# Four of eight first loads split into 120 and 8 partitions, in a kernel of windowed attention and a gated MLP block

## The chip, the core and the metric

The kernel runs on one core of a Trainium2 chip. The metric is the time of one execution on the device in microseconds (us): before the change 156.29, the median of three runs (155.95 to 157.16).

A core has five instruction streams. TensorE (PE) multiplies matrices and also transposes them against an identity. VectorE (DVE), ScalarE (ACT) and GpSimd (POOL) do elementwise work; GpSimd also issues transfers that convert float32 to bf16 on the way. SyncE (SP) does nothing here but issue plain transfers. All transfers, whoever issues them, are carried by the same sixteen DMA engines.

## What is computed

Attention in which each row sees the first four positions (the sinks) and a window of 128, then a gated MLP in which a 768x768 matrix mixes the positions:

```python
B, H, S, D = 4, 8, 768, 64
scores = q @ k^T / sqrt(D)
keep = (pos_k < 4) | (0 <= pos_q - pos_k < 128)
a = softmax(where(keep, scores, -1e9))
x = (a @ v)                         # heads side by side: (4, 768, 512)
h = gelu_tanh(x @ w_in)             # 512 -> 1024
u, v = h[..., :512], h[..., 512:]
v_n = layernorm(v) * g_ln
v_s = w_sg @ v_n + b_sg             # over the 768 positions
out = x + (u * v_s) @ w_out
```

## The kernel before

The order of all work is written out by hand, in one long list of steps (STEPS); each name calls a small function, its numbers say for which batch and tile, and a last letter says on which engine. Each engine runs its own steps in that order. A step starts when its engine has reached it and its inputs are there. The four batches overlap: while the MLP of one batch runs, the attention of the next is mixed in. Steps on PE that wait for nothing (WARM and HM.n, n products of a tile of zeros) fill its early gaps.

The change touches the loads of q and k of the first batch. They come as plain float32 transfers issued by SP, one for each pair of heads: LPQ.g and LPK.g, g from 0 to 3. Each moves 128 partitions times two heads times 384 numbers: 256 pieces of 1,536 bytes, 393 KB. Within one transfer a partition holds six neighbouring positions of two heads. The pairs 0 and 1 lie in the tile uT, the pairs 2 and 3 in the tile z, which are free at that time. SP's own order is q0, k0, k1, q1, q2, LG (g_ln, four partitions), k2, k3, q3, and then LC: four small transfers that fetch the sink rows of v into the tile vs, eight partitions each. After them SP has nothing to do until the transposes of the second batch.

What follows each load: a cast to bf16 (CPQ and CPK; ACT for q0, k0 and k2, GpSimd for k1 and k3, DVE for q1, q2 and q3), transposes on PE (TQ and TK), a copy out of PSUM (EQ and EK on ACT or DVE), the scores (QK), the exponentials (EX), the masks (MK) and the product with v (AV), which is normalised by NR. On GpSimd the cast of k1 stands ahead of LVH.0.0 and LVH.0.1, the two transfers that bring v of the first batch; the cast of k3 follows, and then the loads of the second batch's q and k and of the weights: LW (w_in), LWS (w_sg), and much later LWO (w_out), first needed by OU, the last product of the first batch. GpSimd's loads of q, k and v write pieces of 128 bytes.

SP's transfers share eight completion counters in turn, so each transfer from the ninth on waits until the one eight places before it on SP has landed. Before the change the ninth is q3, which waits for q0; then the four transfers of LC wait for k0, k1, q1 and q2. GpSimd's transfers have eight counters of their own.

Of the kernel before, what the change touches and what calls it, by code (L numbers as in the profile page):

```python
# [14 lines left out]
HOW = "GBBC"  # L15
VHOW = "HHHH"
BIG = 1e9


STEPS = """  # L20
# [55 lines left out]
def kernel(  # L76
# [14 lines left out]
    nc = tc.nc  # L91
# [48 lines left out]
    z = Ring("z", 2, [128, NT, d_half], BF16)  # L140
# [96 lines left out]
    def pair(key, g):  # L237
        both = uT.get(("f", g)).rearrange("p c s -> p (c s)") if g < 2 else z.get(("f", g)).rearrange("p t d -> p (t d)")
        i = "qk".index(key)
        return both.bitcast(F32)[:, S * i:S * (i + 1)]  # L240

    def load_pair(key, src, g):
        return nc.sync.dma_start(out=pair(key, g).rearrange("p (h f) -> p h f", h=2),
                                 in_=src[0, 2 * g:2 * g + 2].rearrange("h (p t) d -> p h (t d)", p=128))

    def LPQ(g):
        return load_pair("q", q, g)

    def LPK(g):
        return load_pair("k", k, g)  # L250
# [78 lines left out]
    def MASK0():  # L329
        nc.vector.tensor_copy(mask0, mask1)  # L330
        nc.vector.memset(mask0[0:n_sink, 0:256], 1.0)
        for m, bias in ((mask0, bias0), (mask1, bias1)):
            nc.vector.tensor_scalar(out=bias, in0=m, scalar1=-1.0, scalar2=BIG, op0=ALU.add, op1=ALU.mult)

# [376 lines left out]
```

## Time and profile before

| | us |
|---|---|
| median of three runs | 156.29 |
| the profiled execution, its time | 157.69 |
| its span, from the first to the last instruction | 156.0 |
| PE busy | 146.7 (94%) |
| DVE busy | 123.4 (79%) |
| ACT busy | 99.0 (64%) |
| GpSimd busy | 99.3 (64%) |
| granted TensorE clock | 1.0 throughout |
| moved by SP's queue | 13.41 MB |
| moved by GpSimd's queue | 11.01 MB |

The profiled execution took 1.69 us more than its own span. A line of the profile names the engine, the source line, the operation, and the tiles as output<-inputs. "Idle before" is how long the engine stood still ahead of an instruction, and the arrow names what ended the wait. A name with a small q behind the engine (SPq) is the engine's sequencer, here issuing transfers. Beside the summary, the trace holds when each transfer's completion counter rose. A transfer over 128 partitions raises its counter sixteen times, once for each DMA engine when its share has landed; these times come without the engine's name, sorted. A transfer has landed with its last count.

### The profile page before, as it was taken

The numbers are of one execution on the slowest core, as the hardware profiler recorded it, in microseconds if no ns is written. First come the engines' busy times: TensorE is split into PE (matmuls) and PEld (weight loads), VectorE is DVE, ScalarE is ACT, GpSimd is POOL, SyncE is SP. The second block draws the span as 40 slices with busy tenths as digits, with TensorE's granted clock in tenths as the row PEclk, the third lists the DMA queues.
The fourth block names the chain that finished last, engine by engine and source line by source line (L and its number), as shares of the span: only waits on it lengthen the run. The fifth ranks groups of instructions, "written<-read, shape, count | busy, mean of one in ns | idle before, by whom it ended". The sixth has DMA issues, their size and how long they took to land.

```text
span 156.0 us, 3856 instructions
## 1 busy us (share of the span) xinstructions
PE 146.7 (94%) x1549; PEld 94.2 (60%) x1549; DVE 123.4 (79%) x295; ACT 99.0 (64%) x110; POOL 99.3 (64%) x127
## 2 busy tenths in 40 slices
PE   6988989999999979989999999999999999999990
PEld 2445577779675756747566764486567644776530
DVE  4557789829989969969789887899789956867981
ACT  3699798799899846276897855269954025591000
POOL 4099779388999899997549869640798610300400
PEclk9999999999999999999999999999999999999999
DMA  4999999999999999999999199995710580510064
GB/s 156 282 365 151 153 197 189 166 192 193 146 143 142 193 152 139 167 156 156 168 230 246 22 285 174 178 197 60 236 71 3 102 235 0 202 63 11 0 227 179
DMA packets 86170, 24.67 MB, mean 158 GB/s; under 512 B 78660, under 2 KB 83016, under 8 KB 86152
## 3 DMA queue, kind: packets, MB, share of 16 engines
q0 software_dynamic: 64608, 11.01, 94.9%
q1 hardware_dynamic: 21544, 13.41, 33.1%
q8 instruction: 12, 0.20, 0.5%
q14 instruction: 6, 0.05, 0.1%
HBM read 24.81 MB, written 6.29 MB: 199 GB/s over the span
## 4 chain that ended last, share of the span: by engine, by line
PE 73%; DMA 17%; DVE 2%; POOL 2%; issue 1%; ACT 1%; SPq 1%; ACTq 0%
PE mm L622 17%; PE mm L639 14%; PE sc L561 13%; PE sc L602 12%; DMA w_out_sb<-in_moe_w_out_dram 7%; DMA v_sb<-in_v_dram 6%; PE sc L478 4%; DMA uT<-in_k_dram 4%; PE mm L519 3%; PE mm L377 3%; PE mm L523 2%; PE mm L526 2%; PE mm L614 1%; POOL v_sb L269 1%; PE mm L545 1%
## 5 line engine op out<-in xcount | busy, mean ns | idle before, releaser
L483 ACT ACTIVATE P<-sc 128x1024 bf16<-128x1024 f32 (+1 forms) x48 | 43.4, 953 | 10.3 <-PE sc L478 10.1
L622 PE MATMUL mm<-wsgT,z 128*128 128x384 bf16 x192 | 34.1, 327 | 0.0
L622 PEld LDWEIGHTS <-z 128*128 128x128 bf16 x192 | 17.7, 98 | 11.9 <-issue 0.7
L639 PE MATMUL mm<-w_out_sb,wsg_gated 128*128 128x512 bf16 x96 | 22.7, 379 | 1.1 <-DMA w_out_sb<-in_moe_w_out_dram 1.1
L561 PE MATMUL sc<-w_in_sb,xT 128*128 128x512 bf16 x96 | 22.2, 379 | 0.7 <-ACT vt L565 0.7
L627 DVE SCALAR_TENSOR_TENSOR gtmp<-mm,g_sb,b_bc 128x384 bf16<-128x384 f32 x32 | 19.1, 611 | 4.2 <-PE mm L622 3.6
L602 PE MATMUL sc<-xT,w_in_sb 128*128 128x256 bf16 x192 | 22.1, 273 | 0.0
L493 POOL TENSOR_SCALAR_AFFINE_SELECT P<-P 128x512 bf16<-128x512 bf16 x21 | 14.0, 667 | 12.3 <-ACT P L483 12.0
L632 POOL TENSOR_TENSOR wsg_gated<-gtmp,uT 128x384 bf16<-128x384 bf16 x15 | 14.5, 982 | 10.9 <-DVE gtmp L627 10.9
L574 DVE BATCH_NORM_STATS2 st<-vt 128x6 f32<-128x512 f32 x24 | 15.4, 685 | 7.5 <-ACT vt L565 7.4
L602 PEld LDWEIGHTS <-w_in_sb 128*128 128x128 bf16 x192 | 18.7, 98 | 3.0
L536 DVE TENSOR_TENSOR x_sb<-mm,rcp 128x384 bf16<-128x384 f32 (+1 forms) x36 | 18.5, 513 | 1.2
L643 DVE TENSOR_TENSOR ot<-mm,x_sb 128x512 f32<-128x512 f32 x24 | 16.1, 684 | 2.7 <-PE mm L639 2.5
L565 ACT ACTIVATE vt<-sc 128x1024 f32<-128x1024 f32 x12 | 12.3, 1027 | 9.0 <-PE sc L561 8.9
L583 POOL TENSOR_TENSOR rs<-rs,neg_half 128x4 f32<-128x4 f32 (+1 forms) x8 | 6.9, 867 | 17.4 <-DVE rs L578 16.0
L223 POOL DMA_DIRECT2D k<-in_k_dram x18 | 16.4, 928 | 0.7 <-DMA v_sb<-in_v_dram 0.7
L223 POOL DMA_DIRECT2D q<-in_q_dram x18 | 16.7, 952 | 0.0
L519 PE MATMUL mm<-v_sb,P 128*128 128x65 bf16 x192 | 15.9, 194 | 0.7 <-DMA v_sb<-in_v_dram 0.6
L519 PEld LDWEIGHTS <-P 128*128 128x128 bf16 x192 | 14.5, 98 | 2.8 <-issue 0.6
L639 PEld LDWEIGHTS <-wsg_gated 128*128 128x128 bf16 x96 | 9.2, 98 | 11.4 <-DMA w_out_sb<-in_moe_w_out_dram 1.4
L561 PEld LDWEIGHTS <-xT 128*128 128x128 bf16 x96 | 9.2, 98 | 10.9 <-issue 0.9
L478 PE MATMUL sc<-qT,kT 64*128 64x128 bf16 (+1 forms) x256 | 14.8, 238 | 0.6 <-DVE qT L198 0.3
(90 smaller groups left out, 244.4 us busy)
## 6 DMA issues: line engine op xcount, KB each, us to landing
out_dram<-ot SPq DMA_DIRECT2D x24, 256.0 KB, 2.3
v_sb<-in_v_dram POOLq DMA_DIRECT2D x8, 384.0 KB, 8.3
q<-in_q_dram POOLq DMA_DIRECT2D x18, 128.0 KB, 6.7
k<-in_k_dram POOLq DMA_DIRECT2D x18, 128.0 KB, 6.9
wsg_gated<-in_moe_w_sg_dram POOLq DMA_DIRECT2D x2, 576.0 KB, 8.3
w_in_sb<-in_moe_w_in_dram POOLq DMA_DIRECT2D x2, 512.0 KB, 10.2
uT<-in_q_dram SPq DMA_DIRECT2D x2, 384.0 KB, 3.2
uT<-in_k_dram SPq DMA_DIRECT2D x2, 384.0 KB
```

Of the source, the lines that this page charges most:

```text
L223: return nc.gpsimd.dma_start(out=dst.rearrange("p (h d) -> p h d", h=H), in_=heads(src, b, i))
L478: nc.tensor.matmul(sc[:, hl, c:c + 128 * ni], at(kT, b)[rows, j, p, :], at(qT, b)[rows, i:i + ni, p, :], start=not biased, stop=(not biase ...
L483: nc.scalar.activation(out=P.new((b, p, g))[:, :, 0:w], in_=sc_ring[b, p, g][:, :, 0:w], func=AF.Exp, scale=scale)
L519: nc.tensor.matmul(av[:, il, hl, :], pt[:, hl, c:c + 128], vb[:, h, i, :], start=first, stop=False)
L536: nc.vector.tensor_mul(x_sb.get(b)[:, i0:i0 + n, 128 * p:128 * (p + 1)].rearrange("p t (h d) -> p t h d", h=2), av[:, :, :, 0:Dh], rcp[:, ...
L561: nc.tensor.matmul(hp[:, jl, :], xT[b][:, 2 * g + jl, c, :], w_in_sb[:, c, d_half:2 * d_half], start=(c == 0), stop=(c == KD - 1))
L574: nc.vector.bn_stats(out=sts[jl], in_=vt[b, g][:, jl, :])
L602: nc.tensor.matmul(hp[:, dc // 2, 256 * (dc % 2):256 * (dc % 2 + 1)], w_in_sb[:, c, 128 * dc:128 * (dc + 1)], xT[b][:, 2 * g:2 * g + 2, c, :],
L622: nc.tensor.matmul(ps[:, 0:NH], z[b][:, si, 128 * dc:128 * (dc + 1)], wsgT[:, si, NH * hf:NH * (hf + 1)], start=(si == 0), stop=(si == NT ...
L627: nc.vector.scalar_tensor_tensor(out=gtmp.new((b, hf, dc)), in0=mm_ring["g", b, hf, dc][:, 0:NH], scalar=g_sb[:, dc:dc + 1], in1=b_bc[:, N ...
L639: nc.tensor.matmul(ps, gated(b, hf)[:, dc, 128 * tl:128 * (tl + 1)], w_out_sb[:, dc, :], start=(dc == 0), stop=(dc == KU - 1))
L643: nc.vector.tensor_add(ot.new((b, t)), mm_ring["o", b, t], x_sb[b][:, t, :])
```

## The change

Four of the eight loads, k1, q1, k2 and q3, are issued as two transfers: partitions 0 to 119, and partitions 120 to 127. The same bytes go to the same places. SP issues four transfers more, and everything behind them in SP's list moves to another of the eight counters. The order of instructions on PE, DVE, ACT and GpSimd is the same; the cast after a cut load waits for two counters instead of one.

```diff
+CUT = (("k", 1), ("q", 1), ("k", 2), ("q", 3))
...
     def load_pair(key, src, g):
-        return nc.sync.dma_start(out=pair(key, g).rearrange("p (h f) -> p h f", h=2),
-                                 in_=src[0, 2 * g:2 * g + 2].rearrange("h (p t) d -> p h (t d)", p=128))
+        dst = pair(key, g).rearrange("p (h f) -> p h f", h=2)
+        rows = src[0, 2 * g:2 * g + 2].rearrange("h (p t) d -> p h (t d)", p=128)
+        cuts = (0, 120, 128) if (key, g) in CUT else (0, 128)
+        for a, z in zip(cuts, cuts[1:]):
+            ins = nc.sync.dma_start(out=dst[a:z], in_=rows[a:z])
+        return ins
```

SP's order after the change, with what each transfer waits for (a is the piece of 120 partitions, b the piece of 8):

| issue | waits for the landing of |
|---|---|
| q0, k0, k1a, k1b, q1a, q1b, q2, LG | nothing |
| k2a | q0 |
| k2b | k0 |
| k3 | k1a |
| q3a | k1b |
| q3b | q1a |
| LC, four transfers | q1b, q2, LG, k2a |

## The prediction, made before the changed kernel ran

> **What bounds the kernel.** PE is busy for 94% of the span, so I first asked where it still stands still, then what ends those waits, then whether the cut loads lie behind them. First the order of time on PE, with idle time in brackets:
>
> ```profile
> 10.93 0.53 PE L371 MATMUL mm<-iden,q 128*64 128x128 bf16 x12 [0.66 <-DVE q L198]
> 15.06 0.56 PE L478 MATMUL sc<-qT,kT 64*128 64x256 bf16 x10 [0.18 <-DVE kT L198]
> 17.67 0.25 PE L519 MATMUL mm<-v_sb,P 128*128 128x65 bf16 x3 [0.21 <-DMA v_sb<-in_v_dram]
> 20.59 0.27 PE L519 MATMUL mm<-v_sb,P 128*128 128x65 bf16 x3 [0.44 <-DMA v_sb<-in_v_dram]
> 56.35 0.82 PE L639 MATMUL mm<-w_out_sb,wsg_gated 128*128 128x512 bf16 x3 [1.15 <-DMA w_out_sb<-in_moe_w_out_dram]
> ```
>
> The reader is to see that transfers end the last three, for v and for w_out. Second, the chain of waits from the start:
>
> ```profile
> 1.81 6.04 DMA uT<-in_k_dram
> 7.84 0.09 issue
> 7.93 0.83 POOL k L202
> 8.76 1.76 POOL v_sb L269
> 10.52 10.03 DMA v_sb<-in_v_dram
> ...
> 45.52 10.79 DMA w_out_sb<-in_moe_w_out_dram
> ```
>
> The cut load k1 heads it: GpSimd casts k1 and only then issues v. Third, SP's issues and DVE's first casts:
>
> ```profile
> 0.79 0.46 SPq L243 DMA_DIRECT2D uT<-in_q_dram  x1
> 3.34 0.41 SPq L290 DMA_DIRECT2D g_rows<-in_moe_g_ln_dram  x1
> 3.79 1.63 SPq L243 DMA_DIRECT2D z<-in_k_dram  x2
> 6.47 4.06 SPq L287 DMA_DIRECT2D vs<-in_v_dram  x4
> ```
> ```profile
> 9.95 0.93 DVE L198 CAST q<-z 128x768 bf16<-128x768 f32 x1 [0.50 <-DMA z<-in_q_dram]
> 13.21 0.93 DVE L198 CAST q<-z 128x768 bf16<-128x768 f32 x1 [1.01 <-DMA z<-in_q_dram]
> ```
>
> SP issues well ahead of the data, and DVE waits for q2 and q3 to land. Last I read the completion counts one by one. Loads land at 8.87 (q1), 9.93, 10.98, 12.00 and 13.19 us (q3): about 1.04 us apart, sixteen packets of 65 ns on each engine. Two engines are late in this row: for q3 fourteen are done by 12.48, the others at 13.09 and 13.19. From there transfers queue without a break. First v piece: the fourteenth count at 15.76, then 16.38 and 17.62. Second: 19.12, 19.32, 20.55. w_out: 54.20, 54.71, 56.31. So each of PE's last three waits is for one late DMA engine. The last engine's extra 1.2 us after 13 fits an instruction packet of 16 KB that one DMA engine carried from 13.80 to 15.06.
>
> **Which engines the pieces use.** The rows have 16 counts for 128 partitions, 8 for the 8-partition transfers of LC, 4 for the 4 of LG: an even split over the most engines that divide the partitions. For 120 that gives 15 engines with eight partitions each, sixteen packets as before, and one engine spared. LC's eight counts show one late engine (12.76, then 13.41; the other three transfers alike, so still at 14.23, after the instruction packet): exactly one of the two late engines is among the eight that a small piece uses, and it is not the one hit by that packet. The one that becomes last is in the other half; I take it to be the one spared. [...] No name of an engine is in this trace.
>
> **The change, part by part.** Issuing: four issues more. Nearest rows 0.41 (LG), 0.46, and 0.60 to 0.75 (LC); I take 0.45 as the form is that of the loads: 1.8 us of SP by q3. The cover is SP's lead: k2 is issued at 3.79 and first wanted when an engine finishes q2, after 8. Without cover it would cost up to 4 x 0.75 = 3.0 us; below nothing it cannot be.
>
> The new waits on SP: k2a and k2b wait for q0 (4.02) and k0 (4.96), when SP gets there anyhow, at some 4.7 and 5.2. k3 waits for k1a, about 7.9, and was issued at 4.23; queued behind it are q3a, q3b and LC. From issue to first packet the first load took 1.2 us (0.79 to 1.95), so k3's packets are there at 9.1; the fastest engine finishes k2 at 9.43. It is covered by 0.3 us there and by 1.9 on the slowest, which is the one that sets the landing. q3a (issued about 8.4) and q3b (8.9, behind q1a) are wanted after 10.5. LC moves from a landing of 14.23 to about 14.8, still before DVE's use of vs at 15.89. So I cost the waits at nothing; if k1a came 2 us later, that cover would be gone and k3 and q3 would slip by the rest.
>
> The second counter of a cast: two counters are read by an instruction that waited for one; no extra instruction. Nothing, bounded by the 0.09 us of the chain's row between landing and cast, four times.
>
> The packets of the small pieces: sixteen over eight engines, 2 x 65 = 0.13 us for each cut load on those eight, 0.52 after four. The late engine among them ends q3 at 13.09 + 0.52 = 13.61 instead of 13.19: 0.42 later. q2: 9.82 + 0.26 = 10.08, 0.15 later. k1: 7.75 + 0.13 = 7.88 against 7.84, so v is issued as before. The bounds: nothing if the other engines speed up when one is idle, 0.52 if not; I take the upper, as 65 ns holds also when few packets move.
>
> The spared engine: 64 packets of 65 ns, 4.16 us of its work gone, more than its lateness anywhere. Then the next engine decides: v at 16.38 + 0.52 = 16.90 and 19.32 + 0.52 = 19.84, 0.7 earlier each, and w_out at 54.71 + 0.52 = 55.23, 1.1 earlier, provided that the head start outlives 40 us of queue.
>
> On PE: q3 being 0.42 late moves DVE's casts and copies and PE's scores, so PE is ready for v at 17.46 + 0.42 = 17.88 rather than running at 17.67: 0.21 lost. It would be ready for the second piece at 20.15 + 0.21 = 20.36, and v is there: 0.23 gained on 20.59. It is ready for w_out at 55.20 - 0.23 = 54.97 and starts at 55.28: 1.07 gained. What is late next is k of the third batch for the transposes at 62.09, landed at 61.76 behind the DMA transposes, which move only with DVE: PE can use 0.33 + 0.23 = 0.56 us. Sum: -0.5 on the span of 156.0. Set against the median (the profiled run was 1.4 above it), 156.29 - 0.5 = 155.8.
>
> **The rivals.** *Nothing reaches the end.* The last engine's lead over w_out has lapsed, or another engine is hit by the instruction packet at 54.28. For it: the gap between last and middle count shrinks from 2.2 us at 17 to 0.4 at 42 and reopens only at w_out. Against: an instruction packet delays one engine and it is the last again. w_out then lands at 56.31, or 56.83 if that engine is among the eight; the 0.23 goes into its wait. 156.3 to 156.8. [...]
>
> *Slower: the 120-piece runs worse.* It goes over eight engines, or its packets run slower than 65 ns because the new split lets engines write in each other's way. Over eight, 30 packets instead of 16: 0.91 us, with the small piece 1.04, four times: q3 4.2 later. For it: no row shows 120 partitions. Against: the divisors of the three rows. PE absorbs 0.21 + 0.44 + 1.15 = 1.8 us in its waits and w_out itself, with 54.71 as base, 1.6; 4.2 - 1.6 gives 158.9. It decides the sign from 0.4 us per cut load on, and passes 1% from 0.8 on (packets of 115 ns). [...]
>
> *Faster by more: k1 lands early.* Its last two engines were at 7.75 and 7.84, the fourteenth at 6.81. If sparing one also frees its fellow, k1, v, q2 and q3 land up to 0.9 earlier and PE's early waits (0.66 and 0.18) go too: 0.84 + 0.64 + 0.33, at most 1.8: 154.5. Against: the late engine in the small pieces' half keeps all its packets.
>
> **How the numbers follow.** The forecast 0.45 (its own range 155.3 to 156.2), nothing reaches the end 0.32, slower 0.14, faster by more 0.09. One per cent, 1.56 us, is what a measurement of this kernel can tell from no change. Over 1% faster needs the last rival nearly whole: 0.06. Over 1% slower needs 0.8 us per cut load, or the same through issues without cover: 0.12. The rest is 0.82. The range runs from part of the early case, 155.0, over the second rival's 156.8 with the runs' own scatter (+0.9 in three) to 157.4; beyond are most of the slower rival and the extreme of the faster.
>
> **What would show it.** k1a has fifteen counts, k1b eight, and one engine's count is missing from the late end. v lands near 16.9 and 19.8, PE's waits at 17.67 and 20.59 go, w_out lands near 55.2, and PE waits for k near 61.6 instead. q3 lands near 13.6. I am wrong if the second count from the end was the same engine in all three groups only by chance, if packets of the large piece take over 65 ns, or if k3 starves an engine.

## The result and the profile after

The changed kernel takes 161.76 us (median of four runs, 160.20 to 162.25) against 156.72 for the kernel before on the same chip: a ratio of 1.031, 95% interval 1.022 to 1.040. It is slower by 3%, where I forecast half a microsecond less. The profiled execution took 160.20 us with a span of 158.5; it is the fastest of the four, the others have spans of 160.0 to 160.5. The medians below are taken over all executions of a run; the ratios leave out those more than 1.5% above the fastest of the same kernel.

First PE's order of time, with its idle time in brackets:

```profile
11.10 0.53 PE L376 MATMUL mm<-iden,q 128*64 128x128 bf16 x12 [0.87 <-DVE q L199]
12.55 0.53 PE L376 MATMUL mm<-iden,q 128*64 128x128 bf16 x12 [0.93 <-DVE q L199]
13.88 0.51 PE L483 MATMUL sc<-qT,kT 64*128 64x256 bf16 x4 [0.27 <-DVE qT L199]
18.27 0.53 PE L376 MATMUL mm<-iden,q 128*64 128x128 bf16 x12 [0.95 <-DVE q L199]
```

The waits for v and for w_out are gone, as forecast, but because PE comes later than they do. What it waits for now are the casts of q1, q2 and q3. The same on DVE, and SP's issues:

```profile
11.48 1.01 DVE L199 CAST q<-z 128x768 bf16<-128x768 f32 x1 [0.44 <-DMA z<-in_q_dram]
17.35 0.87 DVE L199 CAST q<-z 128x768 bf16<-128x768 f32 x1 [3.52 <-DMA z<-in_q_dram]
```
```profile
4.29 3.90 SPq L248 DMA_DIRECT2D z<-in_k_dram  x3
8.23 1.69 SPq L248 DMA_DIRECT2D z<-in_q_dram  x2
10.09 3.77 SPq L292 DMA_DIRECT2D vs<-in_v_dram  x4
```

The cast of q3 starts at 17.35 instead of 13.21. SP's third issue to z, k3, starts at 7.80, right after k1a's landing at 7.78. The chain of waits now leads through q1a and the two pieces of q3:

```profile
2.70 6.93 DMA uT<-in_q_dram
9.65 7.61 DMA z<-in_q_dram
17.30 0.04 issue
17.35 0.87 DVE q L199
18.21 0.87 DVE kT L199
```

Read alone, this chain accuses SP: q3b is issued only when q1a has landed. But the engines are not short of work. The busy times by stretch (us, then PE, PEld, DVE, ACT and GpSimd busy, the granted clock, the DMA engines' share, and GB/s) show how fast they work. Before:

```profile
6.00:10.00 4.00, 3.79 (x57) 1.88 (x56) 2.04 (x9) 3.04 (x4) 2.07 (x2) 1.00 1.00 354
```

After:

```profile
6.00:10.00 4.00, 3.96 (x47) 1.85 (x45) 1.44 (x7) 2.75 (x4) 1.76 (x2) 1.00 1.05 240
```

The DMA engines are busy throughout in both (shares of 1.00 and 1.05), at 354 GB/s and at 240. The packets themselves are slower. Of the loads' 2,048 packets of 1,536 bytes half took at most 65 ns before and nine tenths at most 68; after, those two figures are 91 and 132, and from 7 to 14 us the median in a microsecond is 94 to 122.

A second profile of the kernel before (run e9_before, below) is the better base for the loss, as its execution was a usual one. Against it, ACT's instructions start 1.8 us later at 11 us, 4.4 from 15 us on, 4.3 at 40 us and 4.25 at the last. All of the loss arises before 20 us.

### The profile page after: what moved, and what is told of

The parts are those of the page before. It is cut to its first block, busy times and chain, and to the rows that moved or that the text cites. A ratio compares the mean times of both kernels' runs of the same rounds, so it can differ in the third digit from the quotient of the medians.

```text
span 158.5 us, 3867 instructions
## 1 busy us (share of the span) xinstructions
PE 148.9 (94%) x1549; PEld 95.3 (60%) x1549; DVE 123.4 (78%) x295; ACT 99.1 (63%) x110; POOL 99.6 (63%) x127
## 3 DMA queue, kind: packets, MB, share of 16 engines
q1 hardware_dynamic: 21572, 13.41, 34.2%
## 4 chain that ended last, share of the span: by engine, by line
PE 64%; DMA 15%; POOL 8%; DVE 5%; issue 3%; ACT 2%; SPq 1%; ACTq 0%; DVEq 0%; POOLq 0%
PE mm L627 15%; PE mm L644 13%; PE sc L566 12%; PE sc L607 10%; DMA v_sb<-in_v_dram 5%; DMA z<-in_q_dram 5%; PE sc L483 5%; DMA uT<-in_q_dram 4%; PE mm L524 3%; POOL q L224 2%; PE mm L528 2%; POOL k L224 2%; POOL P L498 2%; PE mm L531 2%; POOL P L501 1%
## 5 line engine op out<-in xcount | busy, mean ns | idle before, releaser
L524 PE MATMUL mm<-v_sb,P 128*128 128x65 bf16 x192 | 16.0, 194 | 0.1
L528 PE MATMUL mm<-v_sb,P 128*128 128x65 bf16 x160 | 15.4, 194 | 0.3 <-POOL P L501 0.3
```

The costliest lines, as they stand in the source:

```text
L524: nc.tensor.matmul(av[:, il, hl, :], pt[:, hl, c:c + 128], vb[:, h, i, :], start=first, stop=False)
L528: nc.tensor.matmul(av[:, il, hl, :], pt[:, hl, c:c + 128], vb[:, h, i - 1, :], start=False, stop=(i < 2 and il == n - 1 and hl == 1))
```

## The experiments

Theory P is a conjecture of mine: a run of neighbouring partitions, split evenly over the DMA engines, makes engines write to the same part of the memory at the same time, so their packets take longer. Rivals: S, the extra issues and waits on SP starve the engines; F, fifteen engines instead of sixteen; the small pieces; the clock. The results together; q3's landing and the packets are from the one profiled execution, GB/s from its stretch 6 to 10 us. The ratio is to the kernel before on the same chip.

| run | us | ratio (95% interval) | packets: half / nine tenths up to (ns) | GB/s | q3 lands (us) |
|---|---|---|---|---|---|
| before | 156.72 | | 65 / 68 | 354 | 13.19 |
| changed | 161.76 | 1.031 (1.022 to 1.040) | 91 / 132 | 240 | 17.25 |
| e1_heads | 156.09 | 0.998 (0.994 to 1.001) | 65 / 68 | 382 | 11.97 |
| e2_112 | 158.90 | 1.015 (1.010 to 1.019) | 81 / 109 | 284 | 14.19 |
| e3_64 | 159.16 | 1.014 (1.010 to 1.018) | 88 / 120 | 261 | 15.93 |
| e4_extra8 | 158.29 | 1.011 (1.008 to 1.015) | 65 / 89 | 339 | 13.66 |
| e5_low64 | 161.69 | 1.031 (1.025 to 1.037) | 75 / 134 | 240 | 17.85 |
| e6_mid64 | 159.39 | 1.015 (1.009 to 1.021) | 65 / 68 | 371 | 14.55 |
| e7_fill | 160.87 | 1.028 (1.021 to 1.035) | 82 / 125 | | 16.11 |
| e8_again | 161.06 | 1.025 (1.020 to 1.030) | 91 / 122 | | 17.21 |
| e9_before | 156.66 | 1.001 (0.997 to 1.005) | 65 / 68 | | 12.86 |
| e10_large | 160.59 | none | 100 / 134 | 251 | 16.94 |
| e14_large | 159.23 | 1.017 (1.011 to 1.023) | 75 / 125 | 264 | 14.35 |
| e11_q3 | 161.52 | 1.027 (1.020 to 1.034) | 65 / 107 | | 14.97 |
| e13_q3 | 158.49 | 1.009 (1.005 to 1.013) | 65 / 108 | 368 | 14.67 |
| e12_k1 | 157.49 | 1.002 (0.998 to 1.005) | 65 / 94 | | 13.91 |

**The same number of issues and waits, cut by head.**

```diff
-        for a, z in zip(cuts, cuts[1:]):
-            ins = nc.sync.dma_start(out=dst[a:z], in_=rows[a:z])
+        for h in range(2):
+            ins = nc.sync.dma_start(out=dst[:, h], in_=rows[:, h])
```

> The same four loads as two transfers each, but one head each over all 128 partitions: as many issues and as many waits on SP as the changed kernel. Theory P (placement: a run of neighbouring partitions sends two DMA engines to the same part of the memory, so packets take about 115 ns instead of 65): packets stay at 65 ns, q3 lands at 13.0 to 13.6 us, time within 1% of before, about 156.7. Theory F (fifteen engines instead of sixteen are the cause): the same. Theory S (the four issues and the waits on SP starve the engines): q3 near 17, about 161.8 us.

156.09 us, no difference that this measurement can tell from before, with q3 at 11.97, earlier than expected; the stretch in its profile:

```profile
6.00:10.00 4.00, 3.55 (x48) 1.79 (x51) 3.28 (x10) 2.86 (x5) 2.77 (x2) 1.00 1.04 382
```

S falls as the first cause: four issues more, and the same shifted waits, cost nothing here (ratio 0.998) with packets that keep their 65 ns. The wait in the chain was a consequence: SP waits for a load that is slow. Once loads are slow, though, the shifted waits can add to the loss, as the next runs show.

**Sixteen engines, other cuts.** In the changed kernel `(0, 120, 128)` becomes:

```diff
-        cuts = (0, 120, 128) if (key, g) in CUT else (0, 128)
+        cuts = (0, 112, 128) if (key, g) in CUT else (0, 128)
```

> The cut at partition 112: both pieces divide by sixteen, seven neighbouring partitions for each engine and then one. P: packets of 90 to 120 ns, q3 lands at 16 to 17.5 us, 159.5 to 162 us. F: packets of 65 ns, q3 at 13.2 to 14, 156.5 to 157.5 us. S: as the changed kernel, 161.8 us, but with packets of 65 ns and gaps between them.

and, in another run, `(0, 64, 128)`:

> The cut at partition 64: two equal pieces, four neighbouring partitions for each of sixteen engines. P: the first piece keeps all engines in one half of the partitions, packets of 115 ns or more, q3 lands at 17 us or later, 161 to 163 us. F: packets of 65 ns, q3 at 13.2 to 14, 156.5 to 157.5 us. S: 161.8 us with packets of 65 ns.

Both are slower by 1.4 to 1.5%, with nine tenths of the packets up to 109 and 120 ns. DVE's casts of q3, of the first and then of the second:

```profile
14.28 0.56 DVE L199 CAST q<-z 128x768 bf16<-128x768 f32 x1 [1.41 <-DMA z<-in_q_dram]
```
```profile
16.03 0.56 DVE L199 CAST q<-z 128x768 bf16<-128x768 f32 x1 [2.17 <-DMA z<-in_q_dram]
```

F falls as the cause: sixteen engines are slow as well. Both stayed below what P expected of the time (159.5 and 161 at least) and of q3's landing (16 and 17), and by the median below its packets (90 and 115 ns), so neighbours in one piece are not the whole account of 120 against 112. In e3_64 one count is late besides: the last of k0, ahead of every cut, comes at 6.35 us where the others are in by 4.97, and that of q3 at 15.93 where they are in by 14.56.

What these two runs wait for is not q3 alone. The chain of both leads through LC, the sink rows of v, which SP issues last. DVE's use of them, before the change and in e2_112:

```profile
15.89 0.68 DVE L352 TENSOR_TENSOR v_sink<-vs,headsel 128x512 bf16<-128x512 f32 x1
```
```profile
18.14 0.99 DVE L357 TENSOR_TENSOR v_sink<-vs,headsel 128x512 bf16<-128x512 f32 x1 [1.46 <-DMA vs<-in_v_dram]
```

The fourth transfer of LC now waits for k2a. In e2_112 that lands at 11.05, LC is issued at 11.08 and lands at 18.11, while the transfers of v move too; before the change it landed at 14.23, ahead of them, and in e1_heads at 13.41. In the changed kernel it lands at 20.04, and DVE takes it up at 20.06 without a wait, as q3 holds DVE up until then.

**Whole loads, and extra pieces that nobody reads.** The extra rows go to the three tiles of the ring `vt`, whose first GELU overwrites them before anything reads them, and to one tile put in the place of the ring `c16`, which this plan does not use. Three runs differ in one line, the extra transfer:

```diff
+        ins = nc.sync.dma_start(out=dst, in_=rows)
+        if (key, g) in CUT:
+            n = CUT.index((key, g))
+            nc.sync.dma_start(out=spare[n][120:128].rearrange("p (h f) -> p h f", h=2), in_=rows[120:128])
```

In e4_extra8 it is as shown. In e5_low64 and e6_mid64 it is, in this order:

```diff
+            nc.sync.dma_start(out=spare[n][0:64].rearrange("p (h f) -> p h f", h=2), in_=rows[0:64])
```
```diff
+            nc.sync.dma_start(out=spare[n][32:96].rearrange("p (h f) -> p h f", h=2), in_=rows[0:64])
```

> All eight loads whole, and after each of the same four a second transfer of partitions 120 to 127 into a tile that nobody reads: issues, waits and small pieces of the changed kernel without its large ones. P: packets of the loads at 65 ns, only the small ones slower, q3 lands at 13.6 to 14.3 us, 156.7 to 157.7 us. F: the same. S: q3 near 17 us, 161.8 us. If the small pieces alone are the cause: likewise q3 near 17 us.

158.29 us, 1.1% slower, q3 at 13.66. That is above the 156.7 to 157.7 expected and more than 0.13 us of packets for each small piece. How much of it is theirs is not shown: in this profile the last count of k0 came at 6.57 where the others were in by 5.00, and PE waited 1.4 us for that.

> All eight loads whole, and after each of the same four an extra transfer of its first 64 rows into partitions 0 to 63 of a tile that nobody reads (half a load more each, 8 packets an engine). Theory P (the slowness comes from which partitions are written at the same time: sixteen engines in the lower half get in each other's way): while the extra pieces move, packets take 100 to 120 ns; q3 lands at 16 to 17.5 us; 158.5 to 161 us. Theory D (it comes from the memory that is read, or from any transfer over fewer than 128 partitions): the same as the next run.

> The same extra transfers of the same 64 rows, written to partitions 32 to 95 instead, so that eight engines write below partition 64 and eight above it. P: packets stay at 65 to 70 ns, q3 lands at 15.0 to 15.8 us (13.2 plus 4 x 0.52), a microsecond or more before the run with partitions 0 to 63; 157 to 159 us. D: packets and landing as in that run.

These two read the same rows in the same number of packets; only the partitions that they write differ. First partitions 0 to 63:

```profile
6.00:10.00 4.00, 3.77 (x47) 1.78 (x47) 0.84 (x7) 2.89 (x4) 2.21 (x2) 1.00 1.09 240
```

then partitions 32 to 95:

```profile
6.00:10.00 4.00, 3.79 (x55) 1.88 (x56) 2.46 (x8) 2.99 (x4) 3.11 (x3) 1.00 1.05 371
```

And DVE's cast of q3, in the same order:

```profile
17.87 0.91 DVE L200 CAST q<-z 128x768 bf16<-128x768 f32 x1 [3.61 <-DMA z<-in_q_dram]
```
```profile
14.58 0.92 DVE L200 CAST q<-z 128x768 bf16<-128x768 f32 x1 [1.96 <-DMA z<-in_q_dram]
```

240 GB/s against 371, q3 3.3 us apart, 161.69 against 159.39 us. This rules out D, by which both runs would be alike: the packets were slower with one choice of the written partitions than with the other (nine tenths up to 134 ns against 68), while the memory that was read and the number of partitions were the same. Why packets into partitions 0 to 63 took longer, no run shows. With partitions 32 to 95 the packets keep their 65 ns and q3 is even somewhat earlier than the 15.0 to 15.8 expected. Both times lie above what P expected (161 and 159 at most). The extra bytes of e6_mid64, four times 197 KB, take 2.1 us at 371 GB/s, and it is 2.7 us slower than before; in its profile DVE waits 1.40 us for the sink rows, which land at 18.69. That the piece of 120, if it gives each of fifteen engines eight neighbouring partitions, is slow for the same reason is inferred from this pair, from its fifteen counts and from its packets (nine tenths up to 132 ns); no run moves the piece of 120 to other partitions with its split unchanged.

**The clock.** In the changed kernel's trace the granted TensorE clock is at half from 13.9 to 17.3 us. Four products of zeros were put ahead of the transposes of q1, q2 and q3:

```diff
-EX.0.0.2 LC CPQ.2.D LVH.0.1 TQ.0.1 MK.0.0.0.D EK.0.1.A TQ.0.2 EQ.0.1.D
+EX.0.0.2 LC CPQ.2.D LVH.0.1 HM.4 TQ.0.1 MK.0.0.0.D EK.0.1.A HM.4 TQ.0.2 EQ.0.1.D
...
-QK.0.1.1.1 EX.0.1.0 LQ.1.0 CPQ.3.D TK.0.2 EX.0.1.1 TK.0.3 EK.0.2.D LQ.1.1 TQ.0.3
+QK.0.1.1.1 EX.0.1.0 LQ.1.0 CPQ.3.D TK.0.2 EX.0.1.1 TK.0.3 EK.0.2.D LQ.1.1 HM.4 TQ.0.3
```

> The changed kernel with four products of zeros on PE ahead of the transposes of q1, q2 and q3, where PE waits 0.9 us each. The trace of the changed kernel shows the clock at half from 13.9 to 17.3 us. If that clock is part of the loss: granted clock 1.0 throughout, and 1 to 2 us less than the changed kernel, about 160. If PE only waits for q3 in that time: no change, 161.8 us, with the clock at 1.0.

The stretch 13.9 to 17.3, in the changed kernel and in this one:

```profile
13.90:17.30 3.40, 3.40 (x36) 1.78 (x35) 0.00 (x0) 2.48 (x4) 2.06 (x3) 0.50 3.20 157
```
```profile
13.90:17.30 3.40, 3.40 (x53) 1.80 (x52) 1.17 (x2) 3.40 (x5) 2.94 (x4) 1.00 3.57 148
```

The clock is whole, and the time is 160.87 us: its interval against before, 1.021 to 1.035, contains both of the changed kernel's ratios, 1.025 and 1.031. In its profile q3 landed 1.1 us earlier than in the changed kernel (16.11), and still nothing was gained: its chain leads through the sink rows, which landed at 20.84 against 20.04, and DVE waited for them:

```profile
20.86 0.70 DVE L357 TENSOR_TENSOR v_sink<-vs,headsel 128x512 bf16<-128x512 f32 x1 [2.29 <-DMA vs<-in_v_dram]
```

So mending the clock alone wins nothing that this run can tell; what the clock would cost without the late loads is not shown.

**Second profiles.** The changed kernel and the kernel before were run again without an edit.

> The changed kernel once more, for a second profile: its profiled run was 160.2 us, the fastest of four. All theories: 160.2 to 162.3 us. If q3 lands later in it than 17.3 us, the spread between its runs is that of the loads; if not, it comes later in the span.

161.06 us, q3 at 17.21, span 158.6: the same picture. The spread of the timed runs (160.3 to 162.8) is not explained by it, as the profiled one was again the fastest.

> The kernel before, for a second profile. 156.0 to 157.2 us. If the profile that the prediction was read from is typical: one engine lands v 1.2 us after the others, PE waits 0.2 and 0.4 us for v and about 1.1 us for w_out. If those waits were that execution's own (it took 157.69 us, above all but one of the timed runs): at least one of them is missing, and a spared engine had less to give than was summed.

156.66 us. PE's waits in this profile, and its first product with w_out:

```profile
11.94 0.34 PE L478 MATMUL sc<-qT,kT 64*128 64x256 bf16 x4 [0.26 <-DVE qT L198]
14.74 0.56 PE L478 MATMUL sc<-qT,kT 64*128 64x256 bf16 x10 [0.18 <-DVE kT L198]
15.46 0.38 PE L188 MATMUL mm<-warm 128*128 128x512 bf16 x1 [0.16 <-issue]
```
```profile
54.06 1.04 PE L639 MATMUL mm<-w_out_sb,wsg_gated 128*128 128x512 bf16 x3
```

The waits for v and for w_out are not there at all. The last engine brings v 0.5 us after the one before it, not 1.2, and w_out lands at 53.56, half a microsecond before PE wants it. The span is 154.5, 1.5 us shorter than that of the profile which the prediction used.

**Large pieces alone, twice.** The small pieces are left out; partitions 120 to 127 of the four loads are cleared, so rows 720 to 767 of two heads each are zeros in q or k. The clearing covers partitions 96 to 127 and stands ahead of the loads, which wait for it (k2 is issued at 5.43 us instead of 3.79), and some steps of GpSimd stand in another order.

```diff
-        for a, z in zip(cuts, cuts[1:]):
-            ins = nc.sync.dma_start(out=dst[a:z], in_=rows[a:z])
+        if (key, g) in CUT:
+            return nc.sync.dma_start(out=dst[0:120], in_=rows[0:120])
...
+            (nc.vector if e == "D" else nc.gpsimd).memset(pair(name[0], int(name[1]))[96:128], 0.0)
```

> The large pieces alone: partitions 120 to 127 of the four loads are cleared instead of loaded (rows 720 to 767 of two heads each are zeros in q or k), so SP has as many issues and waits as before the change. If the large pieces carry the loss: packets of 90 to 120 ns while they move, q3 lands at 15.5 to 17 us, 160 to 161.5 us. If the small ones carry about half: q3 at 14.3 to 15.3, 158 to 159.5 us. If the small ones carry it all: packets of 65 ns, q3 at 13, 156.7 us.

160.59 us is the median of four executions of 158.16, 159.90, 161.27 and 251.31 us, too scattered for an interval; q3 at 16.94. So it was run again:

> The large pieces alone, once more (partitions 120 to 127 of the four loads cleared instead of loaded). If the large pieces carry the loss: q3 lands near 17 us again and the time is 159.5 to 161 us. If the small pieces carry half of it: 158 to 159 us.

159.23 us, 1.7% slower, between the two expectations, and q3 at 14.35, not near 17. By the time the large pieces carry over half of the loss; if all of the 1.1% of e4_extra8 is put down to the small pieces, the sum is 2.8%, between the 2.5 and 3.1% of the changed kernel. Both profiles show the slow packets:

```profile
6.00:10.00 4.00, 2.85 (x36) 1.26 (x32) 2.02 (x10) 2.45 (x4) 2.20 (x3) 1.00 1.08 251
```
```profile
6.00:10.00 4.00, 3.79 (x51) 1.83 (x48) 2.97 (x12) 2.83 (x5) 2.50 (x3) 1.00 1.06 264
```

**One load cut.** `CUT = (("q", 3),)`, twice, and `CUT = (("k", 1),)`.

> Only q3, the last load, is cut. Theory P: each cut costs its own load about 1 us, so q3 lands at 13.9 to 14.5 us; PE's waits for v absorb 0.6 of it and the wait for w_out the rest: 156.5 to 157.5 us, within 1% of before. If the loss were one of the whole stream (SP's waits, the clock), one cut of the last load would cost nothing.

161.52 us (one execution took 296.99), as much as four cuts, but this profile is unlike all others: products with w_out took 391 ns on PE, not 380, and PE's instructions fall behind evenly over the whole span, long after the loads. It decides nothing and was repeated:

> Only q3 cut, once more. Theory P, load by load: products on PE at 380 ns as elsewhere, q3 lands at 14 to 15 us, 157 to 158.5 us. If one cut of the last load costs as much as four: 160 us or more with products of 380 ns.

158.49 us (eight executions of 157.50 to 160.72), 0.9% slower, products at 379 ns. The packets keep 65 ns until q3 moves and take 110 ns then; DVE's casts of q2 and q3:

```profile
9.48 0.93 DVE L199 CAST q<-z 128x768 bf16<-128x768 f32 x1 [0.50 <-DMA z<-in_q_dram]
14.77 0.73 DVE L199 CAST q<-z 128x768 bf16<-128x768 f32 x1 [3.03 <-DMA z<-in_q_dram]
```

Of the loads of q and k only the cut one is late.

> Only k1 is cut, the load at the head of the chain. P: k1 itself lands up to 1 us later and all behind it 0.6 to 1 us later, q3 at 13.8 to 14.3 us, v later by as much: 156.7 to 158.2 us.

157.49 us, not to be told from before, inside the range expected. q3 lands at 13.91, at the lower end, and v at 17.86 and 20.78. The packets' median is 81 and 107 ns in the two microseconds from 5 to 7 us, in which k1 moves, and 65 to 68 after. The loss grows with the cuts, and the one at the end of the loads costs more than the one at their head.

## Why the prediction was wrong

**The step that failed** is the one on engines and packets: "For 120 that gives 15 engines with eight partitions each, sixteen packets as before". The engines were right: k1a's counter rose once at 2.44 us, before any data, and then fifteen times, k1b's eight times. Sixteen packets is right as well, if the 240 of a large piece are spread evenly over the fifteen engines. What I carried over without a row was their duration of 65 ns, which I took for a property of the engine ("as 65 ns holds also when few packets move"). It changed with what the engines wrote at the same time: with extra pieces into partitions 0 to 63 nine tenths of the packets took up to 134 ns (e5_low64, 240 GB/s), into 32 to 95 up to 68 (e6_mid64, 371 GB/s). With medians of 94 to 122 ns from 7 to 14 us q3 landed 4.06 us later (17.25 against 13.19), not 0.42. Packets over 65 ns had been named as a sign of being wrong, but no price was summed for them.

**The rival that came true** was "the 120-piece runs worse", with a chance of 0.14. Of its two variants it was the second, slower packets, and it named packets of 115 ns as the point from which the loss passes 1%. The 4.2 us by which it put q3 later was worked out for the first variant, eight engines, which k1a's fifteen counts rule out; that 4.06 was measured is luck. Its time, 158.9, was too low, because of the next point.

**What PE's waits could absorb, or give.** Both the gain that I summed (0.23 and 1.07 us) and the 1.6 us that the rival was let off were waits of one profiled execution. In e9_before they do not exist. So there was next to nothing to gain, and of the 4.4 us by which q3 is later than in that profile (17.25 against 12.86) 4.25 stay to the last instructions of PE and ACT. The profile had a warning: the profiled execution took 157.69 us where the runs lay between 155.95 and 157.16. I noted it and still summed its waits.

**The issues and waits on SP**, costed at nothing: right for the loads. Small pieces took 0.27 to 0.34 us to issue (k2b 0.58) instead of the 0.45 taken, k3 was issued at 7.80 (about 7.9 said), q3a at 8.23, q3b at 9.65, and in e1_heads such a queue cost nothing (ratio 0.998), with packets of 65 ns. The cover of k3 was not needed, as everything ahead of it was late too. For LC it was wrong: the sink rows landed at 20.04, not at about 14.8, and so after the 15.89 at which DVE had used them. In the changed kernel q3 hides that all but wholly (DVE waits 0.24 us for them in e8_again, not at all in the first profile); in e2_112 and e7_fill it costs the waits of 1.46 and 2.29 us shown above.

**The second counter of a cast** was said to need no extra instruction. The changed program has 3,867 instructions instead of 3,856; four of the eleven are issues, the other seven wait for counters. The cast of q3 starts 0.10 us after the landing instead of 0.02, as it does in e1_heads, which is not slower: the bound of 0.09 us for each was about right.

**The small pieces**, 0.13 us for each on eight engines: probably too low, by e4_extra8, but how much of its 1.1% is theirs is not isolated.

**The spared engine.** That it was the late one, from which the earlier landings of v and w_out were summed, no run shows, as no trace names an engine: v's last two counts are now 20.37 and 20.41 and, for the second piece, 22.79 and 23.14, where the last had been 1.2 us behind, but in e9_before, without a cut, it was only 0.5 behind. What its 4.16 us of saved work can have left is a lead of 0.8 us on the first piece of v (first counts 16.82 and 17.62; in e8_again 17.09 and 17.24) and none at w_out (56.45 and 56.46). A head start that ends where an engine has to wait for the next transfer to be issued would explain this; no run tests it. The gain at w_out, which was summed on that lead, would have failed as well.

**Range and chances.** 157.4 as the upper end left out the slower rival's own time, 158.9. With no row for the piece of 120 partitions, 65 ns and the 115 ns of that rival deserved more even chances.

**What stays open.** It is open why 120 costs more than 112 or 64. In k2a, q1a and q3a four counts come about 1 us after the other eleven (k2a: 11.91, then 12.97 to 13.25); no theory tried here gives four. That the large pieces are slow for the same reason as the extra pieces of e5_low64 is argued, not shown. It is also open why the timed runs of the changed kernel mostly have spans 1.5 us or more above its two profiles.

## What to carry to other kernels

A transfer's packet time, read from whole loads, need not hold for a part of the partitions (median 65 ns before, 91 after): cut loads along the bytes within a partition, which cost nothing here (ratio 0.998), rather than between partitions (1.014 to 1.031 with four loads cut). When the time of a transfer depends on a shape that no row shows, treat the row's duration as one bound and not as the forecast. Before summing the idle times of one profile as a gain, see whether that execution was a usual one. When a transfer is put later on its queue, ask what will be moving by then: the sink rows landed 6 us later for it (20.04 against 14.23).

## What the runs showed of the hardware

- From 6 to 10 us sixteen DMA engines moved 371 GB/s with whole loads and extra pieces into partitions 32 to 95 (e6_mid64), and 240 GB/s with the same extra rows into partitions 0 to 63 (e5_low64).
- A piece of 120 partitions raised its counter fifteen times as data landed and one of 8 eight times; each counter also rose once before any data (for k1a at 2.44 us).
- The granted TensorE clock fell to half for 3.4 us (13.9 to 17.3) after four microseconds in which PE was busy for half the time (0.75 and 1.18 of 2 us each, from 10 to 14 us). With products of zeros in the waits it stayed whole (1.00 in the same stretch of e7_fill), and the time hardly changed (160.87 us against 161.76 and 161.06).
